# A fused attention, dense and routed feed-forward kernel: first decays loaded from the input, and w_out decoded like w_in

## The chip, the core and the metric

The kernel runs on one core of a Trainium2 chip. The metric is the device time of one execution in microseconds (us), the median of several runs. A core has the engines TensorE (PE in the profile, with its weight loads as PEld), VectorE (DVE), ScalarE (ACT) and GpSimd (POOL), a queue that issues transfers (SP, or SPq), and 16 DMA engines. Every engine takes its own instructions in the order in which they were written out, so an instruction that waits holds up all that stand behind it on its engine.

## The reference, cut to what matters

```python
# 1. state-space attention, 4 batches x 8 heads x 768 steps, head_dim 32, d_state 16
log_a = np.log(np.clip(a, 1e-06, 1.0))
# per chunk: decays L = exp(cum_i - cum_j) below the diagonal, then
M = einsum(Cc, Bc) * L
y = einsum(M, xc) + einsum(Cc, state) * exp(cum)
# 2. dense layer on the 3072 rows of 256
h = x @ w_in                                     # 256 -> 2048, weights drawn as float64
g = np.maximum(h, 0.0) + alpha * np.minimum(h, 0.0)
x = g @ w_out                                    # 2048 -> 256
# 3. routed layer: the best of 8 experts per row, 256 -> 1024 -> 256
out[mask] = gate_w[mask, None] * (np.maximum(x[mask] @ w1[e], 0.0) @ w2[e])
```

The kernel gets `w_in` and `w_out` as the 64-bit patterns of float64 and turns them into float32 itself; its matmuls use a rounded high part and a low part of each operand.

## The kernel before

The 3072 rows are 24 chunks of 128 (`SIZES` groups them into 9 blocks of 2 or 3 chunks; 6 chunks are one batch). The span has three stages: an early stage, up to about 150 us, in which the weights are decoded, attention runs for blocks 0 to 3, and the dense layer runs for blocks 0 to 2; a middle stage, written out slot by slot, with the dense layer of blocks 3 to 8 and the attention of the next block beside it; and the routed layer. Only the early stage is touched by the change. Its instructions are ordered by a scheduler, which weighs them by a model of its own; the code gives the order in which it sees them and the priorities. A change of one step can therefore move others on every engine.

Attention of a chunk c: `load_chunk` (line 179) loads `ab`, the decays of 8 heads by 128 steps, to all 128 partitions at once (512 KB are written, 4 KB read), and what the scores need. For chunks under `NEXACT` = 5 that is `bc` from the input. For later chunks it is `bs`, B and C split into three bf16 parts, which are stored in HBM as `bcs` by `split_group` (line 245: 4 subtractions of a 128x1024 tile on DVE with `rbc`, 6 casts, 6 stores) and loaded back by three copies with a leading repeat of 3, 3 and 2 (line 192), one with a leading repeat of 2 (line 194), and one of 32 plain rows (line 195). `attn_a` (line 259) runs a scan over `ab` on DVE (line 264) and the score matmuls; `attn_b` multiplies the two (`mt`, line 286); `attn_c` and `attn_d` make the output `py`, the state `S`, and the halves `xh`, `xl` that the dense layer reads. `ab` has two buffers, `bs`/`bc` two, so a load for chunk c waits for the readers of chunk c-2. A table `GATE` puts the scan of chunk 6 behind the decode of the seventh piece of w_in in the scheduler's order; chunk 7 has no such entry that takes effect, and its scan stands ahead of that of chunk 6 on DVE.

The decays go through HBM once: `a_raw` is loaded, clipped to 1e-6..1, its first column set to zero, and stored as `a_scr` (lines 654 to 657), from which every chunk's `ab` is read.

Weights: `load_wi` and `load_wo` (lines 380, 385) load 8 pieces each of 512 KB into `raw` (four buffers, shared with `rbc`). `from_f64` (line 392) decodes a piece: `m` takes the high word's size with ACT, then a clamp on DVE, `q` takes bits of the low word with ACT, and two DVE operations (lines 411, 412) join them. For w_out the sign of the second layer's input, `sgn`, is put in at this place: `m` is made in two halves by ACT (line 402) and clamped in two halves by DVE (line 403), each with limits per row of `f64s`, which 4 small operations prepare (lines 667 to 670). `conv_wo` (line 421) then takes the rounded copy `wo_h` with one ACT cast (line 424) and `wo_l` with one DVE subtraction (line 425, in the trace under the helper's line 159).

Dense layer: a unit is one block with one of 16 slices of the hidden layer: 6 matmuls to `ph`, `t` on ACT (line 607), `g` on DVE (line 609), the split of `g` into `gh` on ACT and `gl` on POOL, and 6 matmuls to `px` four units later. 48 units make up the early stage. 250 small matmuls (`pw`) fill TensorE's time at the start.

Of the kernel before, what the change touches and what calls it, by code (L numbers as in the profile page):

```python
# [8 lines left out]
F32 = mybir.dt.float32  # L9
# [10 lines left out]
P = 128  # L20
# [32 lines left out]
EARLY = [0 if i < full_pages(2) else 1 if i < N_KNOWN else 2 for i in range(NPAGE)]  # L53
NEXACT = 5
NPH = 3
NM = 2
# [56 lines left out]
def ssm_moe_moe_kernel(  # L113
# [41 lines left out]
    def f(ap):  # L155
        return ap.bitcast(F32)

    def vsub(o, x, y):
        nc.vector.tensor_tensor(o, x, y, ALU.subtract)  # L159
# [19 lines left out]
    def load_chunk(c):  # L179
        ab = ap_.tile([P, NH, P], F32, tag="ab", name="ab", bufs=2)  # L180
        nc.sync.dma_start(ab.rearrange("p h i -> p (h i)"),
                          a_scr[c * NH:(c + 1) * NH].rearrange("h i -> (h i)").partition_broadcast(P))
        if c < NEXACT:
# [148 lines left out]
    def ensure_loaded(c):  # L332
        while nload[0] <= min(c, NCH - 1):
            g, r = divmod(nload[0] + 2 - NEXACT, 8)
            if r == 0 and g > 0 and NEXACT + 8 * g < NCH:
                split_group(g, parts[-1], "part")
            load_chunk(nload[0])
            nload[0] += 1
# [32 lines left out]
    sal = cp.tile([P, KF], F32, name="sal")  # L371
    f64s = cp.tile([P, 3, KF], F32, name="f64s")
    idt = cp.tile([P, NCH], I32, name="idt")
# [18 lines left out]
    def from_f64(raw, tag, g, flip=False):  # L392
# [5 lines left out]
        m = cv.tile([P, 512], F32, tag="m", name="m", bufs=NM)  # L398
        if flip:
            for k in range(2):  # L400
                s, r = slice(k * DM, (k + 1) * DM), slice(2 * g + k, 2 * g + k + 1)
                nc.scalar.activation(m[:, s], H[:, s].bitcast(F32), AF.Abs, scale=f64s[:, 0, r])
                nc.vector.tensor_scalar(m[:, s], m[:, s], f64s[:, 1, r], f64s[:, 2, r], ALU.max, ALU.min)
        else:
            nc.scalar.activation(m, H.bitcast(F32), AF.Abs, scale=F64_SC)
            nc.vector.tensor_scalar(m, m, F64_LO * F64_SC, F64_HI * F64_SC, ALU.max, ALU.min)
        m = m.bitcast(I32)
# [13 lines left out]
    def conv_wo(g):  # L421
        o = from_f64(raws.pop(("o", g)), "wf", g, True).rearrange("p (k d) -> p k d", k=2)
        s = slice(2 * g, 2 * g + 2)
        nc.scalar.copy(wo_h[:, s], o)  # L424
        vsub(wo_l[:, s], o, f(wo_h[:, s]))

# [223 lines left out]

    nc.sync.dma_start(cst, const)
    nc.vector.memset(zero, 0.0)
    nc.vector.tensor_copy(id8, ident[:, None, :].to_broadcast([P, NH, P]))
    nc.sync.dma_start(a_raw, a_rows.rearrange("(p r) i -> p r i", r=2))
    nc.vector.tensor_scalar(a_raw, a_raw, 1e-6, 1.0, ALU.max, ALU.min)
    nc.vector.memset(a_raw[:, :, 0:1], 0.0)
    nc.sync.dma_start(a_scr.rearrange("(p r) i -> p r i", r=2), a_raw)
    load_block(0)
    ensure_loaded(1)
    load_wi(0)  # L660
    load_wi(1)
    load_wo(0)
    nc.sync.dma_start(al, alpha)
    nc.vector.tensor_scalar(sgn, al, 1.0, -2.0, ALU.is_gt, ALU.mult)
    nc.vector.tensor_scalar(sgn, sgn, 1.0, None, ALU.add)
    nc.vector.tensor_tensor(sal, sgn, al, ALU.mult)
    nc.vector.tensor_scalar(f64s[:, 0], al, 1.0, 2.0 ** 32, ALU.is_gt, ALU.mult)
    nc.vector.tensor_scalar(f64s[:, 0], f64s[:, 0], 1.0, F64_SC, ALU.max, ALU.mult)
    nc.vector.tensor_scalar(f64s[:, 1], f64s[:, 0], F64_LO, None, ALU.mult)
    nc.vector.tensor_scalar(f64s[:, 2], f64s[:, 0], F64_HI, None, ALU.mult)  # L670
    nc.sync.dma_start(idwg[:, :, P:], w_gate.rearrange("(k p) e -> p k e", p=P))
# [534 lines left out]
```

## Time and profile before

| | |
|---|---|
| median of 3 runs | 602.78 us (599.75, 602.78, 603.46) |
| profiled execution | 600.14 us, of which the span is 598.3 us |
| busy share of the span | PE 92%, PEld 86%, DVE 73%, ACT 53%, POOL 40% |
| granted clock of TensorE, mean | 0.95 |
| moved by DMA | 92.15 MB, mean 154 GB/s |

The profile divides the span into 40 slices of 15 us, and gives busy time, waits and single instructions with their start. Queries answer for any stretch: busy time by engine, groups of instructions by line and shape, waits by what ended them, and the instructions in order of time. The early stage is the first ten slices.

### The profile page before, as it was taken

What the parts mean: (1) busy time and instruction counts of PE and PEld (TensorE: products, weight loads), DVE (VectorE), ACT (ScalarE), POOL (GpSimd) and SP (SyncE); (2) the same over time, 40 slices, a digit from 0 to 9 for tenths busy, and PEclk for the clock granted to TensorE, in tenths of its full rate; (3) what the DMA queues carried; (4) which work ended last, traced back from release to release, by engine and by line L of the source; (5) the groups of instructions that cost most, each with busy time, mean ns of one, the idle gap of its engine ahead of it and who ended that gap; (6) DMA issues with size and microseconds to landing.
All of it is one profiled execution on the core that took longest, in us unless ns stands there. A gap on an engine that the chain in (4) does not pass through costs nothing. (4 is left out here: it accounts for less than half of the span.)

```text
span 598.3 us, 12098 instructions
## 1 busy us (share of the span) xinstructions
PE 549.2 (92%) x4271; PEld 515.5 (86%) x4271; DVE 437.9 (73%) x861; ACT 319.0 (53%) x702; POOL 242.0 (40%) x258
## 2 busy tenths in 40 slices
PE   7988785999879999989999999997959999999993
PEld 7867575799768899979999999997959999999993
DVE  4998797963787777778766777488549777877860
ACT  0563664565564354464444444564537677767761
POOL 1143353655435654845845746454004122211211
PEclk9785797999999999999999999997979999999998
DMA  7977654520145226225234200631997976777400
GB/s 231 285 256 222 208 179 148 167 89 1 36 135 171 96 85 182 78 86 180 92 101 145 84 24 22 204 134 35 276 315 248 331 242 218 214 233 230 144 25 7
DMA packets 60563, 92.15 MB, mean 154 GB/s; under 512 B 5102, under 2 KB 37040, under 8 KB 60496
## 3 DMA queue, kind: packets, MB, share of 16 engines
q1 hardware_dynamic: 56974, 82.83, 44.3%
q0 software_dynamic: 2400, 6.32, 2.9%
q10 hardware_dynamic: 1122, 2.16, 1.3%
q8 instruction: 36, 0.59, 0.4%
q14 instruction: 31, 0.25, 0.2%
HBM read 75.59 MB, written 15.96 MB: 153 GB/s over the span
## 5 line engine op out<-in xcount | busy, mean ns | idle before, releaser
L618 POOL TENSOR_TENSOR gl<-g,gh 128x384 fp32r<-128x384 f32 (+1 forms) x144 | 146.8, 1023 | 147.0 <-ACT gh L616 144.6
L607 ACT ACTIVATE t<-ph,sgn 128x384 f32<-128x384 f32 (+1 forms) x144 | 78.5, 546 | 121.2 <-PE ph L153 105.2
L609 DVE SCALAR_TENSOR_TENSOR g<-ph,sal,t 128x384 f32<-128x384 f32 (+1 forms) x144 | 81.1, 566 | 69.8 <-ACT t L607 69.0
L153 PE MATMUL ph<-xh,wi_h 128*128 128x384 f32 (+1 forms) x288 | 100.0, 349 | 14.6 <-DVE g L609 14.4
L153 PE MATMUL px<-gl,wo_h 128*128 128x384 f32 (+1 forms) x288 | 94.9, 330 | 1.7 <-POOL gl L618 1.7
L153 PE MATMUL px<-gh,wo_h 128*128 128x384 f32 (+1 forms) x288 | 94.6, 329 | 1.8 <-ACT wo_h L424 1.4
L153 PE MATMUL px<-gh,wo_l 128*128 128x384 f32 (+1 forms) x288 | 94.0, 327 | 0.0
L153 PE MATMUL ph<-xl,wi_h 128*128 128x384 f32 (+1 forms) x288 | 93.1, 324 | 0.3 <-DVE xl L159 0.3
L153 PE MATMUL ph<-xh,wi_l 128*128 128x384 f32 (+1 forms) x288 | 93.0, 323 | 0.0
L616 ACT CAST gh<-g 128x384 fp32r<-128x384 f32 (+1 forms) x144 | 67.4, 469 | 17.3 <-DVE g L609 17.1
L877 POOL DMA_INDIRECT out_dram<-ob,xr x26 | 28.1, 1080 | 111.3 <-ACT ob L876 65.9
L153 PEld LDWEIGHTS ph<-xh,wi_h 128*128 128x128 f32 x288 | 55.6, 194 | 19.9 <-DVE g L609 16.7
L854 ACT ACTIVATE rh<-ph 128x256 fp32r<-128x256 f32 (+1 forms) x112 | 41.6, 371 | 54.0 <-PE ph L153 53.2
L855 DVE SCALAR_TENSOR_TENSOR rl<-ph,rh 128x256 fp32r<-128x256 f32 (+1 forms) x112 | 45.2, 403 | 23.5 <-ACT rh L854 22.5
L153 PEld LDWEIGHTS px<-gl,wo_h 128*128 128x128 f32 x288 | 56.4, 196 | 3.2 <-POOL gl L618 2.1
L153 PEld LDWEIGHTS px<-gh,wo_h 128*128 128x128 f32 x288 | 56.7, 197 | 2.3 <-ACT wo_h L424 1.6
L153 PEld LDWEIGHTS px<-gh,wo_l 128*128 128x128 f32 x288 | 56.5, 197 | 0.2 <-DVE wo_l L159 0.2
L153 PEld LDWEIGHTS ph<-xl,wi_h 128*128 128x128 f32 x288 | 55.9, 194 | 0.8 <-DVE xl L159 0.5
L153 PEld LDWEIGHTS ph<-xh,wi_l 128*128 128x128 f32 x288 | 55.8, 194 | 0.0
L153 PE MATMUL ph<-x2h,wi_h 128*128 128x256 f32 x144 | 41.7, 290 | 5.6 <-DVE rl L855 5.6
L964 DVE TENSOR_TENSOR_SCAN ab<-ab,id 128x512 f32<-128x512 f32 x30 | 44.2, 1475 | 0.0
L569 POOL DMA_INDIRECT srt<-xr,pi x24 | 25.7, 1072 | 43.5 <-DVE sets L695 30.5
(149 smaller groups left out, 1306.5 us busy)
## 6 DMA issues: line engine op xcount, KB each, us to landing
raw<-in_w_dram SPq DMA_DIRECT2D x56, 512.0 KB
ab<-a_scr SPq DMA_DIRECT2D x24, 512.0 KB
srt<-zr SPq DMA_DIRECT2D x8, 645.0 KB
raw<-in_w_in_dram SPq DMA_DIRECT2D x8, 512.0 KB
raw<-in_w_out_dram SPq DMA_DIRECT2D x8, 512.0 KB
bs<-bcs SPq DMA_DIRECT2D x38, 96.0 KB
bs<-bcs SPq DMA_DIRECT2D x19, 192.0 KB
xr<-srt SPq DMA_DIRECT2D x14, 258.0 KB
```

The costliest lines, as they stand in the source:

```text
L153: nc.tensor.matmul(o, l, r, start=start, stop=stop)
L569: sc = nc.gpsimd.indirect_dma_start(out=srt[:, :], out_offset=bass.IndirectOffsetOnAxis(ap=pi[:, t:t + 1].bitcast(U32), axis=0), in_=xr[:, ...
L607: nc.scalar.activation(t[:, :N], ph[:, :N], AF.Copy, scale=sg)
L609: nc.vector.scalar_tensor_tensor(g[:, :N], ph[:, :N], sal[:, fc:fc + 1], t[:, :N], ALU.mult, ALU.max)
L616: nc.scalar.copy(gh[:, :N], g[:, :N])
L618: nc.gpsimd.tensor_tensor(gl[:, :N], g[:, :N], f(gh[:, :N]), ALU.subtract)
L854: nc.scalar.activation(rh[:, :n], ph[:, :n], AF.Relu)
L855: nc.vector.scalar_tensor_tensor(rl[:, :n], ph[:, :n], 0.0, f(rh[:, :n]), ALU.max, ALU.subtract)
L877: nc.gpsimd.indirect_dma_start(out=out[:, :], out_offset=bass.IndirectOffsetOnAxis(ap=xr[:, t, ROW - 1:ROW].bitcast(U32), axis=0), in_=ob, ...
L964: nc.vector.tensor_tensor_scan(lt[:, s_].rearrange("p h i -> p (h i)"), lt[:, s_].rearrange("p h i -> p (h i)"), id8[:, s_].rearrange("p h ...
```

## The change

Decays: chunks 0 and 1 (`NDIRECT` = 2) read `ab` straight from the input rows, and DVE clips the 128x1024 tile and zeroes the first column of each head after the load. The trip through `a_scr` stays for the other chunks. The constants are loaded in two parts, the identity first, and the order of the first loads is written anew.

Weights: w_out goes through the same decode as w_in, whose clamp limits are constants; `f64s` and its operations are gone. `conv_wo` now works slice by slice, with ACT's scale and a DVE operation of three operands that multiply by `sgn`.

```diff
+NDIRECT = 2
...
     def load_chunk(c):
         ab = ap_.tile([P, NH, P], F32, tag="ab", name="ab", bufs=2)
+        src = a_rows if c < NDIRECT else a_scr
         nc.sync.dma_start(ab.rearrange("p h i -> p (h i)"),
-                          a_scr[c * NH:(c + 1) * NH].rearrange("h i -> (h i)").partition_broadcast(P))
+                          src[c * NH:(c + 1) * NH].rearrange("h i -> (h i)").partition_broadcast(P))
+        if c < NDIRECT:
+            nc.vector.tensor_scalar(ab, ab, 1e-6, 1.0, ALU.max, ALU.min)
+            nc.vector.memset(ab[:, :, 0:1], 0.0)
...
-    f64s = cp.tile([P, 3, KF], F32, name="f64s")
...
-        if flip:
-            for k in range(2):
-                s, r = slice(k * DM, (k + 1) * DM), slice(2 * g + k, 2 * g + k + 1)
-                nc.scalar.activation(m[:, s], H[:, s].bitcast(F32), AF.Abs, scale=f64s[:, 0, r])
-                nc.vector.tensor_scalar(m[:, s], m[:, s], f64s[:, 1, r], f64s[:, 2, r], ALU.max, ALU.min)
-        else:
-            nc.scalar.activation(m, H.bitcast(F32), AF.Abs, scale=F64_SC)
-            nc.vector.tensor_scalar(m, m, F64_LO * F64_SC, F64_HI * F64_SC, ALU.max, ALU.min)
+        nc.scalar.activation(m, H.bitcast(F32), AF.Abs, scale=F64_SC)
+        nc.vector.tensor_scalar(m, m, F64_LO * F64_SC, F64_HI * F64_SC, ALU.max, ALU.min)
...
         o = from_f64(raws.pop(("o", g)), "wf", g, True).rearrange("p (k d) -> p k d", k=2)
-        s = slice(2 * g, 2 * g + 2)
-        nc.scalar.copy(wo_h[:, s], o)
-        vsub(wo_l[:, s], o, f(wo_h[:, s]))
+        for k in range(2):
+            fc = 2 * g + k
+            sg = sgn[:, fc:fc + 1]
+            nc.scalar.activation(wo_h[:, fc], o[:, k], AF.Copy, scale=sg)
+            nc.vector.scalar_tensor_tensor(wo_l[:, fc], o[:, k], sg, f(wo_h[:, fc]), ALU.mult, ALU.subtract)
...
-    nc.sync.dma_start(cst, const)
     nc.vector.memset(zero, 0.0)
+    nc.sync.dma_start(cst[:, :C_MASK], const[:, :C_MASK])
+    ensure_loaded(0)
     nc.vector.tensor_copy(id8, ident[:, None, :].to_broadcast([P, NH, P]))
+    load_block(0)
+    ensure_loaded(1)
+    nc.sync.dma_start(cst[:, C_MASK:], const[:, C_MASK:])
+    load_wi(0)
     nc.sync.dma_start(a_raw, a_rows.rearrange("(p r) i -> p r i", r=2))
...
     nc.sync.dma_start(a_scr.rearrange("(p r) i -> p r i", r=2), a_raw)
-    load_block(0)
-    ensure_loaded(1)
-    load_wi(0)
     load_wi(1)
+    nc.sync.dma_start(al, alpha)
     load_wo(0)
-    nc.sync.dma_start(al, alpha)
...
-    nc.vector.tensor_scalar(f64s[:, 0], al, 1.0, 2.0 ** 32, ALU.is_gt, ALU.mult)
...
```

The scheduler's order moves at three places. The first is the start of the program on SP, the transfers in the order of issue. In the kernel before (the number behind a name tells buffers apart; `ab_129` and `ab_134` are the decays of chunks 0 and 1):

```order
L651 DMA cst_78<-in_const_dram 128x841
L654 DMA a_raw_95<-in_a_rows_dram 96x256
L210 DMA xt_121<-in_x_nat_dram 128x2x256
L212 DMA bn_123<-in_b_nat_dram 128x2x128
L215 DMA ct_125<-in_c_t_dram 128x256
L218 DMA ad_127<-in_a_rep_dram 128x256
L186 DMA bc_131<-in_bc_x_dram 16x1024 x2
L657 DMA a_scr_79<-a_raw_95 96x256
L186 DMA bc_136<-in_bc_x_dram 16x1024 x2
L181 DMA ab_129<-a_scr_79 128x1024
L181 DMA ab_134<-a_scr_79 128x1024
L382 DMA raw_139<-in_w_in_dram 128x2x256
```

And the same place on SP in the changed kernel (`ab_115` and `ab_131` are chunks 0 and 1):

```order
L653 DMA cst_78<-in_const_dram 128x128
L184 DMA ab_115<-in_a_rows_dram 128x1024
L192 DMA bc_119<-in_bc_x_dram 16x1024 x2
L216 DMA xt_123<-in_x_nat_dram 128x2x256
L218 DMA bn_125<-in_b_nat_dram 128x2x128
L221 DMA ct_127<-in_c_t_dram 128x256
L224 DMA ad_129<-in_a_rep_dram 128x256
L184 DMA ab_131<-in_a_rows_dram 128x1024
L192 DMA bc_135<-in_bc_x_dram 16x1024 x2
L658 DMA cst_78<-in_const_dram 128x713
L387 DMA raw_139<-in_w_in_dram 128x2x256
L660 DMA a_raw_95<-in_a_rows_dram 96x256
```

The decays of chunk 0 are now the second transfer instead of the twelfth, those of chunk 1 the ninth, and the first piece of w_in has the store of `a_scr` behind it instead of ahead.

The second place is on SP in the middle of the early stage, around the loads for chunk 7. In the kernel before (`ab_1018` and `bs_1020` belong to chunk 6, `ab_1212` and `bs_1214` to chunk 7, `raw_1163` is the last piece of w_in):

```order
L181 DMA ab_1018<-a_scr_79 128x1024
L195 DMA bs_1020<-bcs_81 32x1024
L382 DMA raw_999<-in_w_in_dram 128x2x256
L388 DMA raw_1001<-in_w_out_dram 128x2x256
L218 DMA ad_1226<-in_a_rep_dram 128x384
L192 DMA bs_1214<-bcs_81 48x1x1024 x2
L192 DMA bs_1214<-bcs_81 32x1x1024
L194 DMA bs_1214<-bcs_81 96x1x1024
L181 DMA ab_1212<-a_scr_79 128x1024
```

The same place on SP in the changed kernel:

```order
L184 DMA ab_1018<-a_scr_79 128x1024
L200 DMA bs_1020<-bcs_81 96x1x1024
L201 DMA bs_1020<-bcs_81 32x1024
L393 DMA raw_1001<-in_w_out_dram 128x2x256
L387 DMA raw_1163<-in_w_in_dram 128x2x256
L198 DMA bs_1214<-bcs_81 48x1x1024 x2
L198 DMA bs_1214<-bcs_81 32x1x1024
L200 DMA bs_1214<-bcs_81 96x1x1024
L201 DMA bs_1214<-bcs_81 32x1024
L184 DMA ab_1212<-a_scr_79 128x1024
```

The pieces of w_in are loaded one step earlier: the last one (`raw_1163`) now stands ahead of chunk 7's loads, and all five `bs` loads of chunk 7 stand ahead of its decays.

The third place is on DVE, where the scans of chunks 7 (`ab_1212`) and 6 (`ab_1018`) stand. In the kernel before:

```order
L159 TENSOR_TENSOR wi_l_97<-q_1006,wi_h_96 128x2x256
L264 SCALAR_TENSOR_TENSOR ab_1212<-ab_1212,id8_91 128x1024
L609 SCALAR_TENSOR_TENSOR g_1157<-ph_1148,sal_103,t_1155 128x256
L159 TENSOR_TENSOR wo_l_99<-q_1102,wo_h_98 128x512
L609 SCALAR_TENSOR_TENSOR g_1191<-ph_1182,sal_103,t_1189 128x256
L411 SCALAR_TENSOR_TENSOR q_1170<-m_1167,q_1170 128x512
L609 SCALAR_TENSOR_TENSOR g_1237<-ph_1228,sal_103,t_1235 128x256
L411 SCALAR_TENSOR_TENSOR q_1306<-m_1301,q_1306 128x512
L412 SCALAR_TENSOR_TENSOR q_1170<-raw_999,q_1170 128x512
L264 SCALAR_TENSOR_TENSOR ab_1018<-ab_1018,id8_91 128x1024
```

The same place on DVE in the changed kernel:

```order
L161 TENSOR_TENSOR xl_823<-py_1114,xh_822 128x2x128
L426 SCALAR_TENSOR_TENSOR wo_l_99<-q_1100,sgn_102,wo_h_98 128x256
L270 SCALAR_TENSOR_TENSOR ab_1212<-ab_1212,id8_91 128x1024
L411 SCALAR_TENSOR_TENSOR q_1170<-raw_999,q_1170 128x512
L270 SCALAR_TENSOR_TENSOR ab_1018<-ab_1018,id8_91 128x1024
L426 SCALAR_TENSOR_TENSOR wo_l_99<-q_1100,sgn_102,wo_h_98 128x256
L610 SCALAR_TENSOR_TENSOR g_1157<-ph_1148,sal_103,t_1155 128x256
```

Between the two scans there stood three `g` of the dense layer; now both scans and two other operations stand ahead of the first of them, `g_1157`.

## Rows read from the trace of the kernel before

**Rows 1.** Page, 40 slices: busy tenths of PE and DVE.

```profile
PE   7988785999879999989999999997959999999993
DVE  4998797963787777778766777488549777877860
```

**Rows 2.** Stretches: us, busy time (instructions) by engine, granted clock, DMA share, GB/s.

```profile
60.00:65.00 5.00, 2.41 (x17) 1.70 (x15) 2.44 (x5) 2.82 (x7) 0.00 (x0) 0.94 0.66 222
...
90.00:95.00 5.00, 0.59 (x6) 0.38 (x4) 1.62 (x1) 0.00 (x0) 0.00 (x0) 1.00 0.57 180
...
120.00:150.00 30.00, 30.00 (x268) 29.15 (x268) 13.90 (x30) 18.45 (x47) 15.89 (x21) 1.00 0.12 44
```

**Rows 3.** Waits in 0 to 120 us: us in total, times, longest.

```profile
ACT m L405 <- DMA raw<-in_w_in_dram: 20.5, 2, 13.7
...
PE ph L153 <- DVE g L609: 11.4, 5, 5.5
...
DVE ab L264 <- DMA ab<-a_scr: 8.5, 2, 4.3
```

**Rows 4.** Instructions in time at the start: start, us, engine, line, [idle before].

```profile
1.22 0.42 SPq L654 DMA_DIRECT2D a_raw<-in_a_rows_dram  x1
...
7.71 0.82 SPq L181 DMA_DIRECT2D ab<-a_scr  x2
...
11.77 2.29 DVE L264 TENSOR_TENSOR_SCAN ab<-ab,id 128x1024 f32<-128x1024 f32 x1 [4.21 <-DMA ab<-a_scr]
...
15.38 2.28 DVE L264 TENSOR_TENSOR_SCAN ab<-ab,id 128x1024 f32<-128x1024 f32 x1
...
15.71 0.68 ACT L405 ACTIVATE m<-raw 128x512 f32<-128x512 f32 x1 [13.66 <-DMA raw<-in_w_in_dram]
...
17.06 0.67 ACT L405 ACTIVATE m<-raw 128x512 f32<-128x512 f32 x1
```

**Rows 5.** Groups by shape, 0 to 130 us: count | busy us, mean ns | idle.

```profile
L607 ACT ACTIVATE t<-ph,sgn 128x256 f32<-128x256 f32 x34 | 15.9, 471 | 7.5 <-PE ph L153 7.3
L609 DVE SCALAR_TENSOR_TENSOR g<-ph,sal,t 128x256 f32<-128x256 f32 x34 | 15.7, 471 | 1.9 <-ACT t L607 1.9
...
L402 ACT ACTIVATE m<-raw,f64s 128x256 f32<-128x256 f32 x16 | 7.6, 525 | 1.3 <-DMA raw<-in_w_out_dram 1.1 <-DVE q L411 0.2
...
L403 DVE TENSOR_SCALAR m<-m,f64s 128x256 f32<-128x256 f32 x16 | 6.9, 459 | 0.0
L159 DVE TENSOR_TENSOR wo_l<-q,wo_h 128x512 fp32r<-128x512 f32 x8 | 6.5, 814 | 0.0
...
L424 ACT CAST wo_h<-q 128x512 fp32r<-128x512 f32 x8 | 4.9, 612 | 2.0 <-DVE q L412 2.0
...
L406 DVE TENSOR_SCALAR m<-m 128x512 f32<-128x512 f32 x8 | 3.4, 424 | 4.4 <-ACT m L405 4.4
```

**Rows 6.** Instructions in time, 80 to 96 us, SP and DVE.

```profile
80.27 2.13 SPq L192 DMA_DIRECT2D bs<-bcs  x3
...
83.15 0.40 SPq L181 DMA_DIRECT2D ab<-a_scr  x1
...
93.38 2.29 DVE L264 TENSOR_TENSOR_SCAN ab<-ab,id 128x1024 f32<-128x1024 f32 x1 [4.29 <-DMA ab<-a_scr]
...
95.58 0.46 DVE L609 SCALAR_TENSOR_TENSOR g<-ph,sal,t 128x256 f32<-128x256 f32 x1
```

**Rows 7.** Stretches with few other transfers beside the bs loads; columns as in rows 2.

```profile
80.20:83.20 3.00, 3.00 (x25) 2.68 (x25) 3.00 (x7) 2.63 (x7) 2.51 (x3) 1.00 0.17 60
...
93.30:96.00 2.70, 0.00 (x0) 0.00 (x0) 2.62 (x3) 0.00 (x0) 0.00 (x0) 0.84 0.17 63
```

**Rows 8.** Instructions in time, 41 to 51 us, DVE and SP.

```profile
41.74 1.36 DVE L159 TENSOR_TENSOR rbc<-rbc,part 128x1024 f32<-128x1024 f32 x1
...
45.31 0.62 SPq L257 DMA_DIRECT2D bcs<-part  x1
...
50.43 0.60 SPq L194 DMA_DIRECT2D bs<-bcs  x1
```

More of the change, by code (lines that the diff above doesn't have):

```diff
@@ L666, in ssm_moe_moe_kernel @@
     nc.vector.tensor_tensor(sal, sgn, al, ALU.mult)
-    nc.vector.tensor_scalar(f64s[:, 0], al, 1.0, 2.0 ** 32, ALU.is_gt, ALU.mult)
-    nc.vector.tensor_scalar(f64s[:, 0], f64s[:, 0], 1.0, F64_SC, ALU.max, ALU.mult)
-    nc.vector.tensor_scalar(f64s[:, 1], f64s[:, 0], F64_LO, None, ALU.mult)
-    nc.vector.tensor_scalar(f64s[:, 2], f64s[:, 0], F64_HI, None, ALU.mult)
     nc.sync.dma_start(idwg[:, :, P:], w_gate.rearrange("(k p) e -> p k e", p=P))
```

## The prediction

> **What bounds the kernel now.** I read the 40 slices first [rows 1]: PE stands at 9 tenths from slice 8 on, with few dips, and below that in the first eight slices, 120 us, where DVE is mostly at 7 to 9. The change lies in these slices. The stretches say the same in figures [rows 2]: from 60 to 65 us DVE is busy 2.44 of 5 us and from 90 to 95 us 1.62, while from 120 to 150 us PE is busy all the time and DVE less than half. So the early stage is paced by DVE up to about 120 us, and PE then works off what DVE let through late. The waits name what stops DVE [rows 3]: it waits 8.5 us for the decays `ab`, in two pieces, the longer 4.3; ACT waits 20.5 us for w_in in two pieces, 13.7 of it at the start, and 6.8 later, which is the stall at 60 us; PE waits 11.4 us for `g` of DVE. Last I read the start [rows 4]: the scan of chunk 0 begins at 11.77 us after 4.21 us of waiting for the load from `a_scr`, the scan of chunk 1 at 15.38, and the first decode of w_in at 15.71.
>
> **The change part by part. The start.** Before, the load of `ab` is issued at 7.71 us and lands when the scan begins at 11.77: 4.1 us, the wait for the stored `a_scr` ahead of it [rows 4]. Now it is the second transfer; the second transfer was issued at 1.22 us before, so chunk 0 lands at 1.2 + 4.1 = 5.3. Chunk 1's load stands behind six small ones, and I put its landing at about 10. Each is clipped: 128x1024 in one operation is not in the trace. The nearest row is the clamp of 128x512 at 424 ns [rows 5]; 0.42 us bounds it below and twice that, 0.85, above, and I take 0.75. The zeroed column is put at 0.1. The second scan then begins at 10.4 + 0.9 = 11.3 instead of 15.38: a lead of **4.1 us**, between 3 and 5. The two clips lie in time in which DVE waited before [rows 4], so they cost nothing there; without that cover they would cost 1.7. w_in is read about 2.5 us earlier, since the bytes ahead of it are nearly the same but do not wait for `a_scr`.
>
> **The decode of w_out.** On DVE 16 clamps of half a piece, 6.9 us, become 8 of a whole piece at 424 ns, 3.4 [rows 5]: 3.5 us less. The four `f64s` operations on 128x16 go; I put each at a third of a clamp of 128x256, 0.15, so 0.6. `wo_l` was 8 x 814 ns = 6.5 us and becomes 16 operations with three operands on 128x256, which the trace has only with a PSUM input, `g`, at 471 ns: 16 x 0.47 = 7.5, or 1.0 us more; half a `wo_l` each would be no more at all. Sum -3.5 - 0.6 + 1.0 = -3.1 us of busy time at the upper price; neighbours overlap by some 70 ns and 20 instructions more or less change that, so I take **-2 us**, with -1 and -4 as ends. On ACT the size `m` falls from 7.6 to 8 x 0.68 = 5.4, and `wo_h` goes from 4.9 to 16 x 0.47 = 7.5 at the price of `t` [rows 4, 5]; that is +0.4 us on an engine that is idle nearly half the time. It costs nothing unless a cast of `wo_h` becomes the last thing that `px` waits for.
>
> Were DVE alone the limit, 4.1 + 2 = 6.1 us would come off. It is not alone.
>
> **What is late next.** The scan of chunk 7 waits 4.29 us for its `ab` at 93.38 us [rows 6]. That load was issued at 83.15 and took over 10 us, against 4.1 for the same bytes at the start. Ahead of it, from 80.27, stand the `bs` loads of the same chunk. While these are under way and little else is, the DMA share is 0.17 [rows 7], or 2.7 of 16 engines, although 60 GB/s are all that moves; again 0.17 from 93.3 to 96 us. So a chunk's `bs` loads occupy two or three engines for some 13 us (80.27 to 93.3), and an `ab` load, which spreads over all, is complete only when its part on these engines is. Loads of chunks 5, 6 and 7 follow each other on them: the large one for chunk 5 is issued at 50.43 [rows 8], and from there to 93.3 are 42.9 us for three such batches of 13 and the weights between. That queue hardly has gaps, and the change does not shorten it.
>
> *A page's rule.* The Trainium skill, DMA: Bandwidth & Descriptors, section Why a DMA increments its semaphore by 16 and not by 1, says that a transfer uses as many engines as divide its outermost dimension, and the lowest-numbered ones. By that rule the loads with a leading repeat of 3, 3, 2 and 2 all meet on the same two engines, as the share of 0.17 suggests, and the head start cannot get past them; by the rows alone each batch could use other engines, which is the first rival below. It speaks against this change, and I follow it because the share and the 42.9 us agree.
>
> So what counts is how much earlier that queue starts. The large load for chunk 5 waits for the stores of `bcs`, the last at 45.31, behind the fourth subtraction of `rbc` at 41.74 [rows 8]. From the second scan to there DVE had 41.74 - 15.38 = 26.4 us. In the new order more decode of weights stands in that stretch (all of two pieces of w_in and one of w_out), which I sum from the durations to about 27.6, so the subtraction comes at 11.3 + 27.6 = 38.9, a lead of 2.8. With a little less waiting for the stores I take 3.3 for the queue, between 2 and 5. Then chunk 7's `ab` lands at 93.3 - 3.3 = **90.0**, although DVE would be there some 6 us sooner than before; the 4.3 us wait grows to about 7.
>
> Then the new order on DVE counts. Before, the next `g` follows the scan by 2.2 us (93.38 to 95.58) [rows 6]. Now a decode step, a second scan and half a `wo_l` stand between: 2.2 + 0.6 + 2.2 + 0.3 = 5.3. So `g` comes at 95.3 instead of 95.58: **-0.3 us**. Behind it about 1.2 us of the saved DVE work remains, and PE, full from 120 us on [rows 2], takes over what it is given: **-1.2**. Sum -1.5 us, on the profiled 600.14: 598.6. The profiled execution is 2.64 below the median of the runs; the mean of the four, 601.53, is 1.4 above it, and I add that: **600.0 us**.
>
> **The rivals.** *The lead is kept.* The `bs` loads of different chunks use different engines, or their queue has gaps that the earlier weights fill. For it: ACT's stall of 6.8 us for w_in before 62 us [rows 3] has the same cause, and the piece of w_in that stalled now stands ahead of chunk 5's loads, so up to 4 us more could go. Against it: the 42.9 us without gaps. Time: 601.5 - 6.1 = 595.4, with the stall gone 592.
>
> *Slower: the decays of chunk 7 land no earlier.* Now the last piece of w_in and a fifth `bs` load stand ahead of them, and the queue's start could be held by a piece of w_in that is issued ahead of it. Then 93.3 + 1.4 (one weight piece more, the step from 15.71 to 17.06 between two decodes [rows 4]) = 94.7, `g` at 100.0 instead of 95.58, and the `ab` of chunk 8, behind the same queue, some 2.5 us late on top: +4.4 + 2.5 = 6.9, or 608.4. It decides from a landing later than 90.3, where the two scans eat the rest. For it: the third place in the order. Against it: everything ahead of the queue starts earlier.
>
> *The change does little even at the start*: chunk 0's `ab` shares the engines with six loads behind it and lands at 8 instead of 5.3. Then the lead is 2 us less, the queue starts 1 us earlier, and the sum is near 0: 601.5.
>
> **How the numbers follow.** Forecast 0.52, little even at the start 0.13, lead kept 0.25, slower 0.10. A measurement here can tell about 1% from no change, 6 us: faster means below 596.8, slower above 608.8. The lead kept falls in faster; the forecast and its weak form lie within 1%; half of the slower case passes 608.8, and as much of the forecast's upper tail: faster 0.25, same 0.65, slower 0.10. The range of 595 to 606.5 leaves out half of the kept lead and most of the slower case, about 0.2; the forecast's own range, from the queue's 2 to 5 us and DVE's -1 to -4, is 597 to 603.
>
> **What would show it.** In the changed profile the second scan starts at 11 to 12 us and the first clamp of w_in at 13 to 14; if not, the start is wrong. DVE's clamps fall to 16 of about 424 ns. The scan of chunk 7 waits 5 to 9 us for `ab` and ends its wait at 88 to 92 us: if it waits under 3, the queue of `bs` is not what I think and the lead is kept; past 93 the slower rival holds. The two scans follow each other with PE idle meanwhile. The end of the early stage, the first full stretch of PE, moves by under 3 us.

## The result, and the profile after

The changed kernel takes 608.61 us (median of four, 607.04 to 610.05), the kernel before beside it 601.95: a ratio of 1.011 with a 95% interval of 1.008 to 1.014. It is slower by 1.1%, where I had said 600.0 and, with 0.65, no change that can be told. 608.61 lies 2.1 us above my range. The profiled execution took 609.73 us, its span 607.9 against 598.3; these two executions lie 9.6 us apart, the medians 6.7.

| | before | predicted | after |
|---|---|---|---|
| second scan begins | 15.38 | 11.3 | 12.53 |
| first decode step of w_in (ACT) | 15.71 | about 13.2 | 13.49 |
| fourth subtraction of `rbc` | 41.74 | 38.9 | 40.37 |
| scan of chunk 7 begins | 93.38 | 90.0 | 94.64 |
| wait of DVE ahead of it | 4.29 | about 7 | 7.46 |
| next `g` | 95.58 | 95.3 | 100.01 |
| end of the early stage (first `pxr`) | 149.5 | moves under 3 | 156.4 |

The slices of PE after, where [rows 1] show those of before: the seventh, about 90 to 105 us, falls from 5 tenths to 3, and the eighth from 9 to 8.

```profile
PE   8978883899888999999999999997969999999993
```

The waits of after in 0 to 120 us (us in total, times, longest), to be read against [rows 3]:

```profile
ACT m L404 <- DMA raw<-in_w_out_dram: 13.6, 4, 5.9
ACT m L404 <- DMA raw<-in_w_in_dram: 13.1, 4, 11.4
...
PE ph L155 <- DVE g L610: 11.3, 2, 11.0
...
DVE ab L270 <- DMA ab<-a_scr: 8.5, 2, 7.5
```

The sum of DVE's waits for decays is 8.5 us as before, but now one of them is 7.5 long. PE's waits for `g` also come to the same total, 11.3 against 11.4, but now they are nearly all one gap of 11.0 where the longest was 5.5. Here is the place, DVE and then PE in order of time (start, us, engine, line, operation; idle before it in brackets):

```profile
86.25 0.94 DVE L426 SCALAR_TENSOR_TENSOR wo_l<-q,sgn,wo_h 128x256 fp32r<-128x256 f32 x1
94.64 2.29 DVE L270 TENSOR_TENSOR_SCAN ab<-ab,id 128x1024 f32<-128x1024 f32 x1 [7.46 <-DMA ab<-a_scr]
96.85 0.67 DVE L411 SCALAR_TENSOR_TENSOR q<-raw,q 128x512 int32<-128x512 int32 x1
97.43 2.29 DVE L270 TENSOR_TENSOR_SCAN ab<-ab,id 128x1024 f32<-128x1024 f32 x1
99.63 0.46 DVE L426 SCALAR_TENSOR_TENSOR wo_l<-q,sgn,wo_h 128x256 fp32r<-128x256 f32 x1
100.01 0.48 DVE L610 SCALAR_TENSOR_TENSOR g<-ph,sal,t 128x256 f32<-128x256 f32 x1
```

```profile
89.25 0.28 PE L155 MATMUL px<-gl,wo_h 128*128 128x256 f32 x1
100.54 0.58 PE L155 MATMUL ph<-xh,wi_h 128*128 128x256 f32 x1 [11.02 <-DVE g L610]
100.92 0.41 PE L155 MATMUL ph<-xl,wi_h 128*128 128x256 f32 x1
```

DVE stands at chunk 7's scan from 87.2 to 94.6, then runs both scans and two other steps, and the first `g` for PE comes at 100.01. The gap also costs clock: the matmul of 128x256 took 0.28 us ahead of it and 0.41 to 0.58 behind it. What the early stage holds up to the first `pxr`, before and after (us, busy us by engine with counts, granted clock, DMA share, GB/s):

```profile
0.00:149.50 149.50, 128.65 (x1118) 114.34 (x1119) 114.42 (x204) 76.90 (x168) 61.14 (x71) 0.87 0.57 179
```

```profile
0.00:156.40 156.40, 131.52 (x1119) 115.47 (x1120) 115.10 (x204) 77.65 (x168) 59.70 (x72) 0.86 0.55 171
```

Of the 6.9 us, PE idles 4.0 (24.9 against 20.9) and is busy 2.9 more for the same work. DVE is as busy as before, 115.10 against 114.42, though I had taken 2 us off it. Another 2.3 us of the 9.6 between the spans appear between the first and the last `pxr` (284.0 against 281.7), where the change touches nothing. In the profiled executions below that leave this stage as it is, it takes 280.6 to 285.2 us, so 2.3 us are within what it varies by; I have no other cause for these.

### The profile page after: what moved, and what is told of

Same layout as the page of the kernel before. It is cut to its first block, busy times and chain, and to the rows that moved or that the text cites. A ratio compares the mean times of both kernels' runs of the same rounds, so it can differ in the third digit from the quotient of the medians.

```text
span 607.9 us, 12095 instructions
## 1 busy us (share of the span) xinstructions
PE 555.1 (91%) x4271; PEld 519.9 (86%) x4271; DVE 438.9 (72%) x861; ACT 319.4 (53%) x702; POOL 239.4 (39%) x258
## 5 line engine op out<-in xcount | busy, mean ns | idle before, releaser
L619 POOL TENSOR_TENSOR gl<-g,gh 128x384 fp32r<-128x384 f32 (+1 forms) x144 | 144.0, 1004 | 143.1 <-ACT gh L617 138.1
L155 PE MATMUL ph<-xh,wi_h 128*128 128x384 f32 (+1 forms) x288 | 101.3, 353 | 14.3 <-DVE g L610 14.1
L876 POOL DMA_INDIRECT out_dram<-ob,xr x26 | 27.6, 1061 | 112.5 <-ACT ob L875 61.8
```

Source lines behind the costliest of these rows:

```text
L155: nc.tensor.matmul(o, l, r, start=start, stop=stop)
L619: nc.gpsimd.tensor_tensor(gl[:, :N], g[:, :N], f(gh[:, :N]), ALU.subtract)
L876: nc.gpsimd.indirect_dma_start(out=out[:, :], out_offset=bass.IndirectOffsetOnAxis(ap=xr[:, t, ROW - 1:ROW].bitcast(U32), axis=0), in_=ob, ...
```

## The experiments

All kernels compute the whole reference. Ratios are to runs of the kernel before on the same chip, with 95% intervals. "Stage" is the start of the first `pxr` in the profiled execution: 149.5 before, 156.4 after.

### The two parts apart

`e1_direct_only` has the new start and the old decode of w_out; `e2_wout_only` the old start and the new decode.

```diff
-        if flip:
-            for k in range(2):
...
-                nc.scalar.activation(m[:, s], H[:, s].bitcast(F32), AF.Abs, scale=f64s[:, 0, r])
...
+        nc.scalar.activation(m, H.bitcast(F32), AF.Abs, scale=F64_SC)
+        nc.vector.tensor_scalar(m, m, F64_LO * F64_SC, F64_HI * F64_SC, ALU.max, ALU.min)
```

This with `conv_wo` as in the change, on the kernel before, is e2; the same taken back on the changed kernel is e1.

> The changed kernel with the old decode of w_out put back: only the start (direct decays, split constants, new order of the first loads) is changed. Theory Q (the bs loads share two or three DMA engines, and chunk 7's decays land behind them): the scan of chunk 7 still waits 5 to 8 us and begins at 93 to 95 us, the scan of chunk 6 stands right behind it, and the time is 605 to 609, nearly all of the loss. Theory W (the new decode of w_out costs the time, by its smaller pieces): the loss goes with the decode, 600 to 603, and the scan of chunk 7 begins before 93 us.

> The kernel before with only the decode of w_out changed; the start is the old one. Theory Q: the second scan stays at 15.4 us, chunk 5's bs loads start where they did, but the scheduler again puts all five bs loads of chunk 7 ahead of its decays, so the scan of chunk 7 begins at 93 to 96 us; the scan of chunk 6 stands four g behind it instead of next to it, so g is not held twice: 600 to 605. Theory W: 606 to 610, as the whole change.

The start alone: 604.29, 1.004 [1.001, 1.008], stage 151.4. w_out alone: 609.81, 1.015 [1.010, 1.020], stage 154.1. Neither gains. The start alone lies between the two theories; w_out alone, by its time, falls in that of theory W and is as slow as the whole change (the intervals overlap), though its scans are apart. DVE in e2:

```profile
95.12 2.29 DVE L264 TENSOR_TENSOR_SCAN ab<-ab,id 128x1024 f32<-128x1024 f32 x1 [5.88 <-DMA ab<-a_scr]
...
97.65 0.48 DVE L604 SCALAR_TENSOR_TENSOR g<-ph,sal,t 128x256 f32<-128x256 f32 x1
...
103.16 2.83 DVE L264 TENSOR_TENSOR_SCAN ab<-ab,id 128x1024 f32<-128x1024 f32 x1
```

DVE waits 5.88 us for chunk 7's decays there, but the next `g` follows 2.5 us behind the scan's start, and the other scan 8.0 us behind it. Up to 80 us PE has done 570 matmuls in e2, against 585 before, so part of its loss lies ahead of this place. So two scans in front of `g` are not needed for a loss of this size; what else the new decode costs these runs don't show.

With the start alone chunk 7's scan begins at 92.88, 0.5 us sooner than before although its second scan begins some 3 us sooner; both scans are close together there too (92.88 and 95.67, the next `g` at 97.87), and yet it is only 0.4% slower. The lead of the start is gone by then, with or without the decode of w_out.

### The `bs` loads spread over all engines

The loads with a leading repeat become plain loads of 16 or 48 rows, in every chunk (`e3_after_bs16`, `e4_before_bs16`) or only in chunks 5 to 8 of the early stage (`e5_after_bs16_early`, `e6_before_bs16_early`), each on the changed kernel and on the kernel before.

```diff
-                nc.sync.dma_start(to[48 * q:48 * q + DS * r, 0], bcs[0, c, q:q + 1].to_broadcast([r, DS, NH * P]))
+                [nc.sync.dma_start(to[48 * q + DS * u:48 * q + DS * (u + 1), 0], bcs[0, c, q]) for u in range(r)]
...
-            nc.sync.dma_start(to[:96, 1], all_c[None].to_broadcast([2, 3 * DS, NH * P]))
+            [nc.sync.dma_start(to[48 * u:48 * u + 48, 1], all_c) for u in range(2)]
```

> The changed kernel with each bs load with a leading repeat cut into as many plain loads of 16 or 48 rows, so that they spread over all 16 DMA engines; the bytes are the same, 11 loads a chunk instead of 5. Theory Q: chunk 7's decays land 4 to 6 us after their issue instead of 12, the wait of the scan of chunk 7 falls from 7.5 us to under 2, ACT's waits for w_in and w_out after 40 us fall from some 12 us in sum to under 4, PE's 11 us wait at 90 to 101 us goes, and the time is 594 to 599. Rival O (the loss comes from the order on DVE, two scans ahead of the next g, whatever lands when): PE still waits 5 us or more there, and the time stays above 604. Rival S (11 issues a chunk hold up SP, and the queue of issues becomes the limit): waits for weights grow, and the time is above 608.

> The kernel before with the same cut of the bs loads; the order on DVE and ACT in the early stage is nearly the same as before. Theory Q: the waits for the decays of chunk 7 (4.3 us) and for the piece of w_in before 62 us (6.8 us) go nearly wholly, and the time falls by 4 to 8 us, to 594 to 598. If the engines of the bs loads did not matter: 600 to 604, with both waits as they were.

> As e3, but only the bs loads of chunks 5 to 8 are cut into plain loads; later chunks keep the five loads. In e3 the early stage ended at 144.3 us instead of 156.3, and two gaps of 4.0 and 3.3 us came in the middle stage, at 161 and 254 us, where eight bs loads were issued one behind another for 6.9 us. Theory Q, with the gaps laid to SP: the early stage ends at 144 to 146 us, the two gaps are gone, and the time is 596 to 600. Rival B (the middle stage gives the gain back for another reason, since it is bound by something that does not start sooner): one of the gaps stays, and the time is 603 to 607.

> The same for the kernel before: e4's early stage ended at 141.3 us instead of 149.4. Theory Q: the early stage ends at 140 to 143 us and the time is 593 to 597. Rival B: 600 to 603.

e3: 606.98, 1.008 [1.005, 1.011], stage 144.4. e4: 600.82, 0.998 [0.996, 1.000], stage 141.4. e5: 599.73, 0.995 [0.991, 0.998], stage 146.6. e6: 593.40, 0.984 [0.979, 0.989], stage 142.2.

e5 and e6 came as expected of theory Q. e3 and e4 missed its times, though the early stage became shorter. Cutting in all chunks shortens it by 12.0 and 8.1 us and gives most of that back: in the middle stage PE stands twice more, for 3.8 and 2.8 us in e3 and for 3.7 and 2.8 in e4. The first of these in e4, SP, DVE and PE:

```profile
157.47 6.89 SPq L192 DMA_DIRECT2D bs<-bcs  x8
...
164.84 0.62 DVE L609 SCALAR_TENSOR_TENSOR g<-ph,sal,t 128x384 f32<-128x384 f32 x1 [3.92 <-ACT t L607]
...
165.52 0.63 PE L153 MATMUL ph<-xh,wi_h 128*128 128x384 f32 x1 [3.74 <-DVE g L609]
```

SP takes 6.89 us to issue eight loads, and PE and DVE go on right behind them. That the issues hold them up is read from the place; with the cut in chunks 5 to 8 alone both gaps are gone. So limited, it gains 1.6% on the changed kernel and 1.6% on the one before (8.9 and 8.8 us by the medians). The `bs` loads are what makes chunk 7's decays late in both. Where a transfer's parts complete is seen in the trace's completion events (counted from the records: issue, number of events, last three landings):

```
after  bs, repeat of 2    81.40   3 events    82.46  92.48  93.20
after  ab, 128 rows       82.61  16 events    86.77  93.93  94.61
e5     ab, 128 rows       81.70  16 events    85.17  85.26  85.71
```

Of the load with a repeat of 2, one event comes right after the issue, two at 92.48 and 93.20; `ab` has 14 parts there by 86.8, and the last two land 0.7 us apart behind that load's two. The Trainium skill, DMA: Bandwidth & Descriptors, section Why a DMA increments its semaphore by 16 and not by 1, says that a transfer uses as many engines as divide its outermost dimension, and the lowest-numbered ones. The trace agrees in number: the load with a repeat of 2 has two late events, two parts of `ab` are late, and with the loads cut none is. Which engines these are it does not tell.

But this takes the same 1.6% from both kernels. The lateness is common to them; it does not by itself tell why the change is slower.

### Which scan stands first on DVE

Chunk 6's decays are there long before chunk 7's, yet DVE has chunk 7's scan first. `GATE` names the decode step behind which the scheduler may place a chunk's scan. `e7_after_scan6_earlier` moves chunk 6 ahead; `e16_after_order_back` changes the entries for 7 and 8; `e17_before_scan6_first` is that same table on the kernel before.

```diff
-GATE = {5: 7, 6: 12, 7: 15}
+GATE = {5: 7, 6: 10, 7: 15}
```

```diff
-GATE = {5: 7, 6: 12, 7: 15}
+GATE = {5: 7, 6: 12, 7: 11, 8: 13}
```

The first is e7, the second e16 and e17.

> The changed kernel with one number of the table GATE changed (chunk 6: 10 instead of 12), so that the scan of chunk 6 stands five g ahead of that of chunk 7 and the next g follows one scan instead of two. Theory of two costs (chunk 7's decays late, and two scans ahead of g): the scan of chunk 7 still waits for its decays and begins at 93 to 95.5 us, the next g comes some 2.7 us sooner after it than in the changed kernel (2.2 to 3 us behind the scan's start instead of 5.4), the early stage ends 2 to 4 us sooner, and the time is 605 to 607. If the order of the scans costs nothing: 608 to 610.

> The changed kernel as it was timed (bs loads uncut), with only the table of e13 (scans behind 15, 19 and 25 g). Theory A: the scan of chunk 7 still begins at 93 to 95.5 us, but g comes 2.2 to 3 us behind its start instead of 5.4, the early stage ends at 150 to 153.5 us instead of 156.3, and the time is 602.5 to 606, against 608.6. If the late decays of chunk 7 alone set it: 607 to 610.

> The kernel before with the table of e16: on DVE the scan of chunk 6 now stands ahead of that of chunk 7, both behind 18 g. In e16 the same table took the changed kernel from 608.6 to 598.6, since the scan of chunk 6, whose decays are there, no longer stands behind that of chunk 7. Theory D (in both kernels DVE was blocked by the late decays of chunk 7 while ready work stood behind; the change made the block longer): the wait of 4.3 us for the decays shrinks to under 1.5, the early stage ends at 143 to 147 us instead of 149.4, and the time is 595.5 to 599.5, level with e16 within 3 us. If only the changed kernel had this block: 601 to 603.

e7: 606.78, 1.007 [1.004, 1.010], stage 156.5: chunk 6's scan went to 81.7, but chunk 7's came at 98.8 after a wait of 5.4 us. The time is in the range that I expected, but the early stage did not become shorter, so nothing follows from it. e16: 598.60, 0.997 [0.994, 1.001], stage 145.5, far below what I expected of it. DVE in e16:

```profile
86.47 2.82 DVE L270 TENSOR_TENSOR_SCAN ab<-ab,id 128x1024 f32<-128x1024 f32 x1
...
89.59 0.47 DVE L610 SCALAR_TENSOR_TENSOR g<-ph,sal,t 128x256 f32<-128x256 f32 x1
...
95.15 2.27 DVE L270 TENSOR_TENSOR_SCAN ab<-ab,id 128x1024 f32<-128x1024 f32 x1
...
110.48 2.29 DVE L270 TENSOR_TENSOR_SCAN ab<-ab,id 128x1024 f32<-128x1024 f32 x1 [1.97 <-DMA ab<-a_scr]
```

The loads are nearly as late as in the changed kernel (the last part of chunk 7's `ab` at 93.87), but chunk 6's scan and a dozen other steps fill the time, and the scan at 95.15 waits for nothing. The stretch from 80 to 101 us before, after and in e16:

```profile
80.00:101.00 21.00, 15.49 (x121) 14.28 (x120) 16.71 (x25) 12.26 (x29) 9.15 (x10) 0.86 0.48 149
```

```profile
80.00:101.00 21.00, 9.98 (x89) 8.71 (x88) 13.54 (x20) 7.78 (x19) 6.35 (x8) 0.83 0.57 163
```

```profile
80.00:101.00 21.00, 17.33 (x155) 14.98 (x154) 20.53 (x33) 11.78 (x29) 10.35 (x12) 1.00 0.61 171
```

PE does 89 matmuls there after, against 121 before, and 155 in e16. By the ratios the table is worth 1.4% in the changed kernel, intervals apart. So in the changed kernel the late decays cost the 1.1% together with an order in which DVE stands at them with other work behind; the cut (e5) and the other order each take the loss away. This is one order against one other: the table also moves chunk 8's scan and what stands around it, and by 80 us e16 had already done 605 matmuls against 596. And it is not the whole of what the change costs: w_out alone (e2) is as slow without the two scans together, and 1.1% remains where the decays are no longer late (below). On the kernel before the same table brings nothing: 602.29, 0.998 [0.995, 1.001], stage 148.6. The wait for `ab` is gone there, but both scans stand close, 93.00 and 97.98, with a wait of 1.8 us for ACT between them, and no `g` starts between 91.2 and 100.7. With this table old and changed kernel are alike, 0.998 and 0.997.

### What the change still costs when the loads are cut

With the cut in chunks 5 to 8 the changed kernel stays 1.1% above the kernel before (e5 and e6, intervals apart). `e8_wout_bs16_early` and `e9_direct_bs16_early` are e2 and e1 with that cut. `e10_wout_sign_on_act` and `e12_after_sign_on_act` put the sign in with ACT instead (e10 on e8, e12 on e5):

```diff
-            nc.scalar.activation(wo_h[:, fc], o[:, k], AF.Copy, scale=sg)
-            nc.vector.scalar_tensor_tensor(wo_l[:, fc], o[:, k], sg, f(wo_h[:, fc]), ALU.mult, ALU.subtract)
+            nc.scalar.activation(o[:, k], o[:, k], AF.Copy, scale=sgn[:, 2 * g + k:2 * g + k + 1])
+        nc.scalar.copy(wo_h[:, s], o)
+        vsub(wo_l[:, s], o, f(wo_h[:, s]))
```

> The kernel with only the decode of w_out changed (e2, where the early stage ended at 154.0 us) and the bs loads of chunks 5 to 8 cut. If the decode cost its 4.6 us through the queue alone: the early stage ends with that of e6, at 140 to 143 us, 593 to 597. If the decode has a cost of its own on DVE or ACT: the early stage ends 2 us or more behind that of e6, 596 to 600.

> Only the start changed (as e1), with the bs loads of chunks 5 to 8 cut. e6 with the old start ended the early stage at 142.1 us with 593.4, e5 with the whole change at 146.5 with 599.7; the part of the start is what stands between. Theory A (order: the new start lets the scheduler put the scans of chunks 6, 7 and 8 ahead of two to three g that stood ahead of them before, and each unit of the dense layer that is late costs PE some 1.5 us at the end): the ninth scan begins sooner than in e6 (103.7), at 99 to 102 us, with 21 g ahead of it instead of 23, the early stage ends at 143.5 to 146 us, and the time is 595 to 598. If the start lost its lead through the queue of the bs loads alone: the early stage ends at 139 to 142 us, and the time is 590 to 593.5.

> As e8 (new decode of w_out, old start, bs loads of chunks 5 to 8 cut), but the sign is put in by ACT on the decoded piece, in place, in two halves, and then wo_h is one cast and wo_l one subtraction of two operands on 128x512, as before the change. Theory B (the three-operand wo_l on SBUF operands is what eats the saving on DVE: 16 operations of 0.61 us mean, 9.3 to 11 us, instead of 8 of 0.81): DVE's busy time on the decode falls by 3 to 4 us against e8, the early stage ends at 140 to 143 us instead of 144.8, and the time is 591 to 595 against e8's 597.4. If the order that the scheduler makes of it, or ACT, costs the time: 596 to 599.

> As e5, with the sign put in by ACT as in e10. Theory B: DVE's busy time to the end of the early stage falls by 3 to 4 us, the early stage ends 1.5 to 4 us sooner than e5's 146.5, and the time is 595.5 to 598.5 against 599.7. If ACT becomes what is waited for: 599 to 602, with waits of DVE and PE for wo_h grown.

e8: 597.37, 0.990 [0.983, 0.996], stage 144.9. e9: 594.79, 0.989 [0.986, 0.992], stage 145.4. e10: 601.14, 0.999 [0.995, 1.002], stage 147.7. e12: 597.39, 0.993 [0.990, 0.995], stage 144.1. e8 came as expected if the decode has a cost of its own, and e12 in stage and time as expected of theory B; e9 ended its stage as in theory A, but its time lies between the two ranges. By the ratios e8 lies 0.6% above e6 and e9 0.5%, but both intervals overlap that of e6, so the 1.1% is not divided by this. e10 missed both ranges: it was to gain on e8 and lies 0.9% above it, the intervals just touching. DVE's busy time up to the 48th `g` fell by 2.9 us as meant, but its idle time rose by 5.7.

### The order, with the loads cut

`e13_after_cut_order_back`, `e14_after_cut_order_sign`, `e15_direct_cut_order_back` and `e18_before_cut_scan6_first` put the table of e16 on e5, e12, e9 and e6. `e11_after_scan8_later` is e5 with one entry more:

```diff
-GATE = {5: 7, 6: 12, 7: 15}
+GATE = {5: 7, 6: 12, 7: 15, 8: 13}
```

> As e5 (whole change, bs loads of chunks 5 to 8 cut), with one entry added to the table GATE that puts the scan of chunk 8 behind 23 g on DVE, as in the kernel before, instead of 20. Theory A: the g come 2 to 4 us sooner from the twentieth on, the early stage ends at 142.5 to 145 us instead of 146.5, and the time is 595 to 598 against e5's 599.7. If the order of that scan costs nothing: within 1 us of e5.

> As e5 (whole change, bs loads of chunks 5 to 8 cut), with the table GATE set so that the scans of chunks 7, 6 and 8 stand behind 15, 17 and 23 g on DVE, as nearly as before the change (15, 18, 23), instead of 15, 16 and 20. Theory A (the order of scans against g is the larger part of what is left of the loss): the early stage ends at 142.5 to 144.5 us and the time is 594.5 to 597.5, against e5's 599.7 and e6's 593.4. If the order is not it: 599 to 601.

> As e13, and the sign put in by ACT as in e12, so that wo_l has two operands again (scans behind 15, 19 and 24 g). Theories A and B together (order, and the price of the three-operand wo_l, are the whole loss): 592 to 595, at or below e6. If something else of the change costs time: 596 or more.

> As e9 (only the start changed, bs loads cut), with the same table (scans behind 15, 18 and 24 g). Theory A: the lead of the start is kept at least in part: the early stage ends at 139.5 to 142.5 us, and the time is 590.5 to 593.5, below e6's 593.4 and e9's 594.8. If the lead is lost elsewhere: 594 to 596.

> The kernel before with the bs loads of chunks 5 to 8 cut (e6) and the table of e16. In e6 DVE still waited 4.0 us once for decays and ended the early stage at 142.1 us. Theory D: once the loads are cut, chunk 7's decays land in time and the order is worth little: 591 to 595, level with e6's 593.4. If order and queue are worth their full 5 us each: 587 to 590.

e11: 598.01, 0.993 [0.990, 0.996], stage 144.8. e13: 599.88, 0.996 [0.994, 0.999], stage 148.2. e14: 593.48, 0.985 [0.980, 0.990], stage 143.8. e15: 594.54, 0.987 [0.981, 0.994], stage 144.7. e18: 597.61, 0.990 [0.985, 0.995], stage 144.2. Three of these missed what I expected (e13, e15, e18 brought nothing), one met it: table and sign together (e14) bring the changed kernel to e6, and e13 and e14 lie apart. The table alone does not, nor does the sign alone (e12 and e5 overlap). e11 lies at the upper end of what I expected, and its interval overlaps that of e5, so it shows no gain. The wait of 4.0 us in e6 that the last expectation names is that of the first scan, at 11.52 us; the scans at 84.54 and 90.80 wait for nothing there.

So the cut and the order don't add up: each brings the changed kernel to about 599 (e5, e16), and both together leave it there (e13). And no single edit explains the 1.1% that the change costs with the loads cut. Each edit lets the scheduler place everything anew; I leave that cost open. The fastest kernel by its median is e6, the one before with the loads of chunks 5 to 8 cut: 593.40, 1.6% faster, with e14 (593.48) level.

## Why the prediction was wrong

**The start: right in kind, but nearly a third of the lead was missing.** The second scan came 2.85 us sooner instead of 4.1, below my bounds of 3 to 5, and at 12.53 it lies outside the 11 to 12 that I gave as a sign. By the completion events chunk 0's decays landed at 6.37 where I had 5.3, and chunk 1's at 10.53 where I had about 10; DVE came to the second clip at 11.50, behind other steps. The clips:

```profile
6.40 0.69 DVE L187 TENSOR_SCALAR ab<-ab 128x1024 f32<-128x1024 f32 x1 [3.02 <-DMA ab<-in_a_rows_dram]
...
11.50 0.85 DVE L187 TENSOR_SCALAR ab<-ab 128x1024 f32<-128x1024 f32 x1
...
12.53 2.29 DVE L270 TENSOR_TENSOR_SCAN ab<-ab,id 128x1024 f32<-128x1024 f32 x1
```

They took 0.69 and 0.85 us, inside my bounds of 0.42 and 0.85, around the 0.75 that I took.

**The failed step: the queue's start.** I took the large `bs` load of chunk 5, issued at 50.43 [rows 8], as the beginning of the queue on the few engines, and put the queue 3.3 us sooner. The load was issued 2.0 us sooner, but landed at 60.97 instead of 59.17, 1.8 us later. SP after, in order of issue:

```profile
43.65 0.39 SPq L393 DMA_DIRECT2D raw<-in_w_out_dram  x1
44.57 0.36 SPq L387 DMA_DIRECT2D raw<-in_w_in_dram  x1
45.05 2.25 SPq L198 DMA_DIRECT2D bs<-bcs  x3
47.47 0.36 SPq L184 DMA_DIRECT2D ab<-a_scr  x1
48.38 0.63 SPq L200 DMA_DIRECT2D bs<-bcs  x1
```

The kernel before issues the first of the three small `bs` loads ahead of that piece of w_out:

```profile
44.40 0.79 SPq L192 DMA_DIRECT2D bs<-bcs  x1
...
46.03 0.41 SPq L388 DMA_DIRECT2D raw<-in_w_out_dram  x1
46.49 1.47 SPq L192 DMA_DIRECT2D bs<-bcs  x2
```

The small loads are on the few engines too, so the queue begins with them and with what is issued ahead of them. After, all three come from 45.05 on, behind a piece of w_out and one of w_in, and the chunk's `ab` now stands ahead of the large load; in the completion events the last small one lands at 55.14 (before 54.43) and the two late parts of `ab` take from there to 56.37. So the queue ended 1.8 us later at chunk 5, though DVE's side was 1.4 us sooner, and its stretch up to the fourth subtraction was 27.84 us where I had 27.6. From there to chunk 7's `ab` it took 33.6 us (60.97 to 94.61), against 34.2 before (59.17 to 93.35): that the change would not shorten it was right. That the wait of 7.46 us is near the 7 that I gave is luck: I had DVE at the scan some 6 us sooner and the landing 3.3 sooner; DVE came 1.9 sooner (87.18 against 89.09), and the landing 1.3 later.

**The two scans on DVE: right, and the price as worked out.** I added 5.3 us from the landing to the next `g`; it was 94.64 to 100.01, 5.4. With my landing of 90.0 this cost nothing, with 94.64 it cost 4.4. The slower rival had the landing at 94.7, `g` at 100.0 and 608.4 us; I gave it 0.10, since everything ahead of the queue started earlier, although it names a piece of w_in issued ahead of the queue's start, which is what came, with one of w_out. That its 608.4 is so near 608.61 is partly luck. Its last term, chunk 8 late by 2.5 us, did not come: that scan began at 110.29, before at 111.06. In its place stand the slower matmuls behind the gap and the 2.3 us that I could not place. And the two scans by themselves do not set what each part costs: the start alone has them close together and loses 0.4%, w_out alone has them apart and loses 1.5%.

**The second failed step: DVE's work.** I took 2 us off and found none: 115.10 against 114.42 up to the first `pxr`. Of that 1.5 are the two clips, which I had counted as hidden; but e2, which has no clips, stands at 114.49. The groups by shape, 0 to 130 us (count | busy us, mean ns | idle):

```profile
L426 DVE SCALAR_TENSOR_TENSOR wo_l<-q,sgn,wo_h 128x256 fp32r<-128x256 f32 x16 | 9.3, 608 | 0.3 <-ACT wo_h L425 0.3
L405 DVE TENSOR_SCALAR m<-m 128x512 f32<-128x512 f32 x16 | 7.6, 476 | 6.2 <-ACT m L404 6.2
L425 ACT ACTIVATE wo_h<-q,sgn 128x256 fp32r<-128x256 f32 x16 | 7.2, 502 | 0.4 <-DVE q L411 0.4
```

The clamps saved 2.7 us (10.3 to 7.6) where I had 3.5, at 476 ns instead of 424, and `wo_l` cost 2.8 more (6.5 to 9.3) where I had 1.0, at 608 ns instead of the 471 of `g`. Ten of the 16 took 0.46 to 0.48 us, which is my price; four took 0.94 to 0.96 and two 0.56 and 0.64, and all six began while GpSimd was at work. Two of the four, with GpSimd's row:

```profile
99.63 0.46 DVE L426 SCALAR_TENSOR_TENSOR wo_l<-q,sgn,wo_h 128x256 fp32r<-128x256 f32 x1
...
123.86 1.82 DVE L426 SCALAR_TENSOR_TENSOR wo_l<-q,sgn,wo_h 128x256 fp32r<-128x256 f32 x2
```

```profile
123.54 1.86 POOL L619 TENSOR_TENSOR gl<-g,gh 128x256 fp32r<-128x256 f32 x2 [1.87 <-ACT gh L617]
```

The Trainium skill, SBUF — State Buffer, section Who interferes with whom, says that a DVE instruction with two inputs in SBUF contends with a GpSimd instruction that reads SBUF, and the second to issue waits. The trace agrees: the six slow ones of the 16 lie under GpSimd work. `g`, my price, has one input in PSUM and stayed at 469 ns. So the price of one alone was right, and the term that I left out is the overlap with GpSimd. Half of the old `wo_l`, 407 ns, which I named as the other price, would have been further off. And what I had said of ACT, that `wo_h` costs nothing unless `px` waits for it last, came about once: PE waited 4.2 us for `wo_h` at 63.60, before 1.4 us at 65.88.

**The end.** I let PE, full from 120 us on, take over what DVE gave it. Up to 80 us the changed kernel is ahead, 596 matmuls against 585 in the stretch from 0; from 80 to 101 it does 32 fewer (89 against 121), and PE, which sets the end of the stage, does not regain them. e16, with 155 there, ends the stage at 145.5.

## What to carry to other kernels

A late transfer costs what stands ready behind the instruction that waits for it: with the decays nearly as late, another order on DVE took the changed kernel from 608.61 to 598.60. So when a change moves instructions, count the ready work behind the longest wait, and price it for a landing a few microseconds to either side of the forecast. Where loads queue on few DMA engines, look for the first load on them and for everything issued ahead of it: here a lead of 2.85 us at the start did not bring that load forward (44.40 us before, 45.05 after), and was gone by chunk 5. And where a scheduler decides, one edit's worth is the worth of one order: with another table of numbers the same change went from 1.1% slower to no difference that can be told. What each part of the change costs by itself stays open here.

## What the runs showed of the hardware

- Behind the loads with a leading repeat of 3 and 2, two of the 16 parts of a 128-row load came 7.8 us after the others (86.8 and 94.6 us; 12.0 from issue to landing). With plain 16-row and 48-row loads in their place (e5, five of them ahead of it and six behind) it landed in 4.0 us (81.70 to 85.71).
- Eight such plain loads took SP 6.89 us to issue in the middle stage of e4; with the cut in every chunk the kernel took 600.82 us, with the cut in chunks 5 to 8 alone 593.40.
- A DVE operation with three operands on 128x256 took 0.46 to 0.48 us, or 0.94 to 0.96 in four of 16 cases beside GpSimd work; in e5 its mean was 716 ns against 608 in the changed kernel, with eight of 16 beside GpSimd work at 0.85 to 1.09.
- I had not put a slower PE into the sum. After the last matmul of 89.25 us PE's clock stood at 0.50 (1.2 GHz) from 96 to 100 us, and at 0.60 on the mean from 100 to 105, when PE was at work again:

```profile
96.00:100.00 4.00, 0.00 (x0) 0.00 (x0) 4.00 (x4) 0.62 (x1) 0.21 (x1) 0.50 0.46 123
100.00:105.00 5.00, 4.46 (x23) 4.13 (x23) 5.00 (x11) 3.52 (x8) 2.56 (x4) 0.60 0.50 147
```
